# W1's gradient with the layer gradient held and u moved, each tile turned afterwards, in a fused backward kernel on one core

## The chip, the core and the metric

The kernel runs on one core of one Trainium2 chip. The time is the device time of one launch in microseconds (us). The core has five engines with queues of their own: TensorE (PE, matmuls; its weight loads stand as PEld), VectorE (DVE), ScalarE (ACT), GpSimd (POOL) and SyncE (SP). SP and POOL are used here almost only to issue DMAs. TensorE writes to eight banks (PSUM), and ACT or DVE copies results out of them.

## The reference

The program returns the output of a gated mix of two layers and its gradients by 14 inputs. L = 2048 rows, D = 448, N = 256, F = 1792:

```
g = sigmoid((x * gate_w).sum(-1))                 # x = u, 2048 x 448
a = y + u * Dskip                                 # y: u convolved with K by FFT, K from A, B, C, log_dt
h = x @ w1 + b1                                   # 2048 x 1792
b = (relu(h) ** 2) @ w2 + b2
out = g * a + (1 - g) * b
grads = vjp(out, all inputs but B_x)(grad_out)
```

The part that is changed is one gradient of the dense layer, that of W1 (448 x 1792): x^T times dh, where dh = 2 relu(h) (db @ w2^T) is the layer gradient, 2048 x 1792, and the sum runs over the 2048 rows.

## The kernel before

Everything is in bf16 with sums in fp32. The convolution is made by matmuls with Fourier matrices in two stages (fwd1, fwd2, inv1, inv2), with turns through DRAM between them; K's powers are built on DVE by doubling (tables), multiplied out by small matmuls (kprod), turned and stored (turn), and read back for the gradients by A, B and C (gradient, with zunit, zq, l1, zq2, l2; then params). The dense layer is worked in 14 tiles of 128 features: pass1 makes h, its square and W2's gradient (dw2), pass2 makes dh and W1's gradient (dw1), and project makes the two projections (y, and the gradient by x) between and after them.

In pass2, for layer tile j: dh of the tile (features by 2048 rows) comes from `layer` and a product on DVE, is stored to DRAM for the second projection, and is turned by `turn_tile` in 16 pieces into `hn`, 128 rows by 16 by 128 features, of which there is one buffer. dw1 of tile j - 1 uses hn before the next turn fills it. It makes four output tiles of (up to) 128 inputs by 128 features: for each of the four, 16 matmuls with u's 128 x 128 piece held and hn's piece moved, 128 columns. The last of the four has 64 inputs. All four lie in one bank, and two copies bring them to SBUF, from where two DMAs per two tiles store them.

The order of all this isn't the order of the code. The code records the operations; neighbouring matmuls of one bank are grouped into tasks up to about 1.3 us by a table of costs (`cost`, `build`); and `read` and `emit` take the tasks in the order that the string ORDER gives, with HANDS saying which engine makes each free copy (A for ACT, V for DVE) and issues each free DMA (S for SP, G for POOL), and BANKS where each result lies in PSUM. Dependences are kept by semaphores. So every instruction has one line in the profile, that of `emit` (L499 before, L501 after), and instructions are told apart by shapes and tiles. All of SBUF that is shared over time is one tile, `arena`.

Names in the profile: `arena` is any buffer in SBUF, `banks` any result in PSUM, `ident` the identity matrix; a matmul's form reads rows*columns of the held operand, then rows x columns of the moved one. A turn is a matmul with the identity, and shows as `banks<-ident,arena`.

Of the kernel before, what the change touches and what calls it, by code (L numbers as in the profile page):

```python
# [28 lines left out]
ARENA = 100544  # L29
# [9 lines left out]
    "wwvRvFwAwevQv-wx7pw07rvS1f1g7s4I1E4M4J4K4L4N4O4P74vKv_w6w2wfwyw3160A7D7Jw8wB7G7E73vOvZwS7K7Fw7wTwU7HwPwg3F1I0z2aw91KwQwk2P7M7L7t7u7v7y7x7z7A7N26"
    "w1wlwo7Iwp7B7Cwq2b4G24wi4F7SwC8bwR1MwmwW7Y7P8c8d7Z4H72wVae7w8ead7Qwuaf2c28aj7O7_w41WwF801U1O1Q2dwjakwnwv8fal7T7Uws7V8Z7-wr2h2e8Y9mwh9n9o9r9qw59s"  # L40
    "9uwt2f7W2g8X7R2i818g2k2Q852R86w_7XwYxc8288xdwD2jxewX4QwEwLwHxs892S83wMx9x0wIapwJ8WwNwOxtxvxuxw8-2Jxx2L2M848_909192932H2Iah8axaxAxBwZxb2Kaoagw-x1"
    "anx2x39495969798xOxP87x52FxRxQx6aixS999a9b9c9ex79d9gwKxT9f9ham9j9i9k9l9w9xx8xzwGxf9taqar9vx4xgatxyxEasav9zauac9p9C9D9AxhxUxi9y2l9Exk9Baw9L2may2G"
    "xFax9Ma4yrxl9FyuazaAysb6aDaC9GaByv9NaEaaytyw9RaFaHaIa5aJ1S9Ha69OaG9SaMxmaKaOaNb7b8xqxj9Q9IaPaQb99Jxrbby8a79Ubabcxo9V9Ky5y6y99Tab9PaSbiaRxpa8xCxD"
    "aTbh2pxnaLaWaUaZbdaYa-9WxGyaycy7bIxHaXaVbH2nxXa9xIb39-yxxK2qbJ9_xLb0b2b19Xa1xMbfxVxWyNxNyOxZbka_bjybx-ydblbmbnbobpbq2oa2brbsbtbvbuyPyhbwbybxbBbz"
    "bAbCyKbEbDbFbG2r2syea0bMbey1bLbNxJyLxYz4y3bOy22Oyfyg0E9Yx_y4ynz1z5z2yjykyAyMz3zkzlbPbQzJz6ypa33I2t9ZylzPzmzKyoy02uyi4T4UyBznb4bRbSbUbXyyyzyqyGzL"
    "zoyCzQyDbVyIzM221YcpbYym3KbTz7dOc4zpc5b5yEbg5tbW5ub-yHc6bKb_c72vyT2NbZyQza20yJ2wyFdPdQ5pcqcrcs5qcxdVc1yRcyctcXySc2cazTcYc95vyZcZcbcuzUc0yUcd5wzb"
    "dUyVcey-zqc_yWy_dWz02B2z0wc3cccfyXztyYzu2Ac8z8z9zczd2Czezf1-2xzgzhd0zXd1zVcjd32yzYd2cgcmd4cvzZcAczzWzrzszzzNcBcDcCzA2DzRzizDzEz-dZzjckcnzvzwzBzC"
    "zFzxch2EzGzH4R4S4X4YcldT5rcizO4VA0A1d-dSdRzyz_coA4A5dX4WA2cEcFcGcIcHcJcLcRcKcMcOdLcNcPcQcS3JcTcVcUcWA6d_e05se2e4d5dNdY3Ld8e3AaAezSe1eIeH4ZA3d6d9"
    "d7eKda4-e7e8e950e6e5dbecBiAfAbdceeAgedAcA75xeb4_51ea5AAhef5y5Cehddei5B5zde58Ajdfdg54Ad555E5FeJ57ejencwc-A9egeo5253565b59dF5Del5G5cdGdHdIdq5geL5f"
    "dhdtdrdidjeMdudv5h5jdk5iemep5Idldm5aerdndK5HekeSeO5LdJ5k5M5JdMdoeqAuesevdwdCetexewds5PdzeTAydD5d5eAzAvAw5oeNA85QeyezfgeBeAeCeQeVeUeWeXeYeZeue-e_"  # L50
    "f4f0f1f2f3f5f7f6f8fadx5l5K5YdpAAAk6a5m68zIAidydA696bABAo5RADf95S5T5UdB5O5nAxeDAlApAqAm666EASfbfcfdAT5Nfe67An5V6FAOAPAQ5ZAUhlArAR5-AV5WBjfffhdEAt"
    "fiflfkfmfofnfqfwft5_frfpeF5Xfufxfsfv61As63fy60AEAFAG646ceEfFfG6v6g6265eGhn6whohpeRhqfzfHfAhthrAWfBfjhvf-huhsAH6fhAePfIhzfLfM6dfJhBf_g0g1g76xfC6y"
    "6h6jg6gxgwgygAfOfD6i6GAIAJfNAXhmfPgBgCg3hxAKfU6ofE6k6n6rfQACAN6e6HfV6p6sfRgEfX6qALfK6KgD6t6LfYAMgFhCBA6I6J8h6z6B6AB9hk6uBCAYB0B1B2AZfZfW6m6N6Og4"
    "g96Cg2g8gagcgbgdge6D8jfS6MfTB5B3hDhygf6lggghgigjgkglgqgmgnBagogpB6BbA-BcB7A_6RB8grgs6SBlg5Bk6PBdhwgtgugviggG0ChFhEgJgHBmB46QBnBUBggIhIgKihiigL6U"
    "6W6VhJgMBeBogNhHhehGhKhNgVgOhLhOhfhghPhShUgzij6ZBphMhThYBqhhhRBfgPhW6ThQBzhXgQgR6Xhjik6-gWh-hV6YgXhZgYirisgSBr8iilg_imBsi0i2i1gTiRBVi570BWh0iniS"
    "iTBtBxh2BviViWh3iX6_BhiYiZhigUh1gZBBBHByg-i6BwBIBXh4h_i3BEBFCgBDi8i7ibiaBLh8BJh5i4i-hbChiphci9h6BuBM8lBGit8niuivixiwiyiziAiBBNBSBQC0C1h9BZBRBTBY"
    "C4C58m8kBPhdBOh7BKCiiCiDB-CBC6C7C2iEB_CfCDiGiFiIC3iHCdiLiJ8UC9iKiMiNCACCCbC8iOiP8o8p8q8w8x8y8rCc8s8z8Vhaio0yCkCejUicCn8AiQjFieid8t8uCoCl8BCY2Tje"
    "8C8vifiqiUCZjfjgjhi_CmCanSobCXj0j5j2j38Ej68F8Gji8D8MGbof8N8Ojzj1Cpj4j7k38PC-nRDg8HjAjBjCjbjDjJnUj8jkjl8QCIjjj98IjmjajcCFCGCJk8k9jdCHnPCjCrCsCqnT"
    "jECtDh8JDiCK8K8RjIohnXnZCwnYCyCvjtn-jnoECuCzju8SCxjooejpn_o0jqnVCEnWCMCNCOo20Bjro1CLCTogk4jXp1k5jYkajZCPDjCVCQCWo3jwo4oFkbo6CUoojvDDo5omj-onCSo7"
    "o8j_jxnQ8ToaopD0CRokjsjyD3oljGk0jHoDD1D4D2DooiDlojDpDmjKoGo9k6k7D5D6DYp2C_D7D8D9DcorDbocoqDnp0osDqotqgDaodDEjLDdjNDFoujMjPjTjRjOjVpTDeDfovjWowoH"  # L60
    "oIDkjSkdoxDsDLoJjQDtkooKk1DroyDuDZDwkgDvkhD-DGkikkDMkjp3kcDyD_keklozDIDBDzDNkfoADJDCDKHyk2kyE1DxE2E3DAE4E5E6EFkrEGktkvkukDkskxkwkEkJknkpkqkFkmkz"
    "oLkAEEoMkTE7oNoBDHDPDQDRoOoPoCoQkGkOkPkBE_kQk-DOpVGlk_oZDTkCDSkRDUDWDXkWkKpUkYkZoUkXDVqFoVkMkSkUEHpSkLoWoRoSp6oToXE0p7kNkHE8oYkIkVl1p8pap4E9Eap9"
    "EhpbEjp5pcpdqhEcEfEgEJEMEkEKENl0EbEOqfEdo-o_pepfEeELEipQpYphp-piqipZq0pgq1l2Elpjp_l3l4EnpWEvEwppqGpmExl5plpkl7pXq2Eol6q3l8pnpRpoldEplbl9q4lcqjEq"
    "Ezq5ErEyEsqklelJlfq6lhqElaqHEtlgq7q8EmlmlllMliq9lQlRlOlnlNlPlolpECqpF0lqEuljFklur2lrqqqlqmlkltEDqnlvlxlwlyqbF1EAlCF7lsFllSF8qoshlBlAlzlFEBEIqamo"
    "lKlTlGEQr4F4lDlEF5qsF9qcFmlIqrqdqwqOqPqBqxqtquF6qMlHqemxqyERqvqIlVqzEPr1ESmyqAqJEXqCqKqNF2lUlYlLr3EYEUlWqDqLEZlZETEVlXForUm0E-mtmrm1m4mumsFGl-qQ"
    "m5Fpm2EWFrFsq-qRmvm3qVmwr9Fqm9rbqSraFam7qTFtrc8Lr5r6m8mambmcmgr7mdqWF3r8m6l_FbrWrTFcFdFiFeqUmfFgmhqXreFhFHmkFIqZmpmen3mimlFjmjrdmzmnmmrRFfsgFNFK"
    "FLFnFvqYmAFwFxq_FOG6FMFzFBsGFyG7FPrVsjFAmBmDmCFCmErirjmIrkr0FErfrgFDrhrXFFmHmJmqmLmKrYr_mMrmmGmFmNrZs1s0Gcr-rlFJFRJQmQs2n6n8namPFSn7n9mTGdmUmRs3"
    "FTrnroFWs4Genbs5mSmXsisdFYmYFZs6FXFUs8mOsFrSs9sas7FVsbGfn4skmZsHslm-sIm_n0soF-smspscrpFQsqF_mVn1pxmWn2nesnFut3nfsrstG0G1ssuincniG2ngnjseG3sxndsN"
    "nhsfsuG8tVG5nlsOsvsyswn5sLsMnnsPsCnmsJsKGmszsAG4t2tUGonqnrnosQsBsRsSsDnpnvnusTsUnynwt4t5sWGpnzsVG9sEnDnxsXtanCnGGGGasYtbnEt6sZnFnstXt8t7nBnHs_nJ"
    "s-nInAtWt9tctdGhujtetfuhGjGwukt0GnGinttStgthtitjtotkpqtltYtZu0prpspyu1t-pwpvpLpKtmpNrqpMt_u2GkGgGzGyptu3pGpupztrpCpDpFpEtnpAtpnkt1GrGDpHu5GuGxu4"  # L70
    "rrGErxrwtTrvtqpBv8pIGsu9pOrLuruarMGtpJupruusrtv7u6uqubu7rsrNu8ultsv9unrDumueuorzrArOucpPrEudGFuGuuutrGGOrytwGBufrFvbrHvdrCGCGPrIrBrKuytvrPtytzuD"
    "uvuwtxtutMrJnLGqGvuztNGRuAuxtEtFuguCuBvattGSuEtItOtPtQtAuHGKuFuMu_v6uNuOv0v1v2v3vcnKuLtJGHuJuIGQtBtHtGGUtLGItCtKtDJRuKuTuUGLrQuPHxH3uXuQv4GTuVuW"
    "H4GNuYGJtRHzH0uRHAHBuSnMH1HCnOH6H2nNGYHDHFGVHGHHHIHEGWHJHMHTHKHUu-HVGZuZG_H5HWJSGXJTGMHXHLHZHhHeH-HYH_I0I1I4HfIbHiIcIdJUIeIfHaHbI2IgHgHSHRGAv5Ih"
    "IiIjHkH7HcI7I3H8IkIlIoIvIaIwIxH9HNI8ImHdHrI5IyIsHuIzIrItIBHjIAHsHvICHPIDIEHQHlIGI6IuI9IFIIIJIKInINHtHmIMILHoG-HwIHIOHnIpIqHOIRIPHpJJHqJIJKJHIQIS"
    "IWIUIVIXJ1J2J3J4IYJ8J5J6J7JfJ9JgJhJiITJaI_J0JmJkJlJnJvJoJjJeJdI-JpJqIZJtJuJyJwJAJzJxJcJrJBJCJDJsJFJEJGJLJMJNJOJbJP")
HANDS = (
    "AAAVGSAAAASSAAAAGSAAAAGSAVAVAVVVAAVAVAVAVVVVAVVVVAAVAAAVAVVAAAVAAAAAGSAAAASGAAAAGSAAAASSVAAAVASAAAASGSSSAVAAVVAVAAAVAAAAAAVVAVAAAAAVAAAAVAAVAASA"
    "AAAAAAAAASSAASSGSAAAAAAAAAASGAASSGSAAAAAAAAAAGSAASGAAAAAAAAAAGGAAGSVAAVAGAGAGASASVSVGAGASASGGGGSSSAGAGASVSVGVSVGAGAVAVVASAGAGASVGVGVGASVGVGAAAAA"
    "AAAAAAAVAVAAVVAVVVVAAAAAVVVVAAAAVGVAAAASAGVSVSASVSAGAGASASVVVAAGAGVSVGVGVSAGAGASAGAAVVAVAAAAAAVVVAAAAVAVVVAAVAAAAAAAAAAAGVAVAAGAGAGVGAGVSASAGASA"
    "SVAVAVSAGAGVSAGAGVSAGASASAAAAAAAAAAAAAAAAAVAAAVVVAAAVVAAAAAAAAVSAVAAVSASVGVSAGVGVSASVSASSSGGVAVVSAAVVSGGAAAVGVAVASGSAAVAGAAAAGSGAAAVGAVAVSGGSGAA"  # L80
# [184 lines left out]
class Order:  # L265
# [95 lines left out]
    def cost(self, it):  # L361
# [5 lines left out]
        if eng == "PE":  # L367
# [5 lines left out]
            if "tile_position" in k:  # L373
                c = max(1, 128 // max(rows, 32 if rows <= 32 else 64)) * (4 if cols <= 32 else 2 if cols <= 64 else 1)
# [146 lines left out]
def kernel(ctx, tc, A_u, A_A_re, A_A_im, A_B_re, A_B_im, A_C_re, A_C_im, A_log_dt, A_Dskip,  # L521
# [39 lines left out]
    def bank(n=1):  # L561
        return order.banks(n)
# [966 lines left out]
```

## Time and profile before

| | |
|---|---|
| three runs | 714.98, 716.46, 716.55 us; median 716.46 |
| profiled execution | 715.82 us, span from first to last instruction 714.0 |
| granted TensorE clock | 0.978 |
| busy | PE 662.6, PEld 409.0, DVE 544.8, ACT 426.6, POOL 155.7 us |
| DMA | 191.42 MB, 268 GB/s |

A busy share is an average over stages; which engine bounds a stage is read from the busy times of that stretch and from the waits in it. A group's mean length is that of one instruction from start to end; matmuls overlap, so a matmul's price in a row is the group's busy time divided by its count.

### The profile page before, as it was taken

How to read it: one execution, taken by the hardware profiler on the slowest of the kernel's cores; microseconds unless marked ns; L12 is line 12 of the kernel's file. 1: busy time of each engine (PE TensorE's matmuls, PEld its weight loads, DVE VectorE, ACT ScalarE, POOL GpSimd, SP SyncE). 2: the span in 40 equal slices, each digit the busy share in tenths (PEclk: the TensorE clock that was granted, in tenths of full speed). 3: DMA queues.
4: the chain of work that ended last, by engine and by line, in shares of the span. 5: the costliest groups of instructions: out<-in, count | busy, mean ns of one | idle time of the engine just before them, and what ended most of it. 6: DMA issues, size and time to landing. Idle time of an engine off the chain costs nothing.

```text
span 714.0 us, 18735 instructions
## 1 busy us (share of the span) xinstructions
PE 662.6 (93%) x7864; PEld 409.0 (57%) x7864; DVE 544.8 (76%) x918; ACT 426.6 (60%) x638; POOL 155.7 (22%) x262
## 2 busy tenths in 40 slices
PE   2876999999999899888999999999999998899997
PEld 1432564655754545436788866775657675564442
DVE  3589978899798798798983775478877879982652
ACT  4599978989778667656531534436573766651012
POOL 3001222130220122133122212311221031333122
PEclk9989979999999899999999999999999999999998
DMA  8946556568788987899989988997988888999796
GB/s 173 259 148 221 194 192 216 202 242 295 252 259 336 336 281 267 279 329 318 374 270 290 285 273 264 351 298 260 303 273 267 246 234 283 293 280 344 263 294 179
DMA packets 94190, 191.42 MB, mean 268 GB/s; under 512 B 18327, under 2 KB 64793, under 8 KB 91417
## 3 DMA queue, kind: packets, MB, share of 16 engines
q0 software_dynamic: 22320, 93.70, 40.2%
q1 hardware_dynamic: 70488, 89.12, 40.2%
q10 hardware_dynamic: 1296, 7.41, 2.5%
q8 instruction: 61, 1.00, 0.6%
q14 instruction: 25, 0.20, 0.1%
HBM read 104.81 MB, written 85.38 MB: 266 GB/s over the span
## 4 chain that ended last, share of the span: by engine, by line
PE 63%; DMA 14%; DVE 8%; issue 6%; ACT 6%; SPq 1%; POOL 1%; POOLq 0%; DVEq 0%; ACTq 0%
PE banks L499 63%; DVE arena L499 8%; ACT arena L499 6%; DMA arena<-in_A_u_dram 3%; DMA arena<-hd 2%; DMA arena<-c_Ek 2%; DMA arena<-yt_d 1%; DMA hd<-arena 1%; DMA arena<-drT_d 1%; DMA arena<-dk_d 1%; DMA arena<-fb_d 1%; SPq L499 1%; DMA yt_d<-arena 1%; DMA arena<-in_A_C_re_dram 1%; POOL arena L499 0%
## 5 line engine op out<-in xcount | busy, mean ns | idle before, releaser
L499 PEld LDWEIGHTS <-arena 128*128 128x128 bf16 (+4 forms) x6798 | 349.4, 106 | 227.3 <-issue 98.9
L499 PE MATMUL banks<-arena 128*64 128x16 bf16 (+11 forms) x5300 | 433.4, 257 | 18.1 <-ACT arena L499 12.6
L499 DVE TENSOR_TENSOR arena<-arena 128x512 bf16<-128x512 bf16 (+11 forms) x526 | 374.6, 749 | 29.9 <-PE banks L499 11.1
L499 ACT CAST arena<-banks 128x896 bf16<-128x896 f32 (+6 forms) x293 | 213.4, 763 | 201.4 <-PE banks L499 169.4
L499 ACT COPY arena<-banks 128x1024 bf16<-128x1024 bf16 (+3 forms) x129 | 115.1, 917 | 51.6 <-PE banks L499 50.5
L499 PE MATMUL banks<-ident,arena 128*128 128x128 bf16 (+2 forms) x1354 | 115.5, 230 | 19.4 <-DMA arena<-in_A_A_re_dram 7.4
L499 DVE CAST arena<-banks 128x448 bf16<-128x448 f32 (+8 forms) x63 | 48.4, 778 | 39.3 <-PE banks L499 27.5
L499 DVE COPY arena<-banks 128x1024 bf16<-128x1024 bf16 (+4 forms) x58 | 35.2, 616 | 45.0 <-PE banks L499 35.8
L499 DVE SCALAR_TENSOR_TENSOR arena<-banks,arena 128x1024 bf16<-128x1024 f32 (+1 forms) x44 | 44.0, 1003 | 20.7 <-PE banks L499 13.7
L499 PE MATMUL banks<-arena,ident 128*128 128x512 bf16 (+2 forms) x352 | 58.3, 294 | 0.0
L499 POOL DMA_DIRECT2D yt_d<-arena x36 | 19.9, 553 | 135.3 <-ACT arena L499 96.4
L499 PE MATMUL banks<-arena,MI 64*128 64x448 bf16 x384 | 43.0, 360 | 2.9 <-DVE arena L499 1.8
L499 ACT ACTIVATE arena<-arena 128x512 f32<-128x512 f32 (+5 forms) x68 | 42.5, 648 | 3.6 <-DVE arena L499 3.6
L499 POOL DMA_DIRECT2D out_dram<-arena x44 | 25.1, 572 | 61.1 <-ACT arena L499 41.1
L499 PEld LDWEIGHTS <-ident 128*128 128x128 bf16 x352 | 26.2, 98 | 19.1 <-issue 6.4
L499 ACT ACTIVATE arena<-banks,pcol 128x1024 bf16<-128x1024 f32 x27 | 29.7, 1131 | 4.0 <-PE banks L499 2.0
L499 PEld LDWEIGHTS <-MI 64*128 64x128 bf16 x384 | 17.6, 96 | 21.3 <-issue 7.3
L499 ACT CAST arena<-arena 128x512 bf16<-128x512 f32 (+2 forms) x52 | 25.2, 503 | 0.4 <-ACT arena L499 0.4
L499 POOL DMA_DIRECT2D arena<-in_B_w_dram x26 | 16.2, 624 | 32.2 <-PE banks L499 31.9
L499 PE MATMUL banks<-arena,negI 128*128 128x512 bf16 (+2 forms) x100 | 22.1, 308 | 0.2 <-DVE arena L499 0.2
L499 PE MATMUL banks<-arena,F 64*128 64x448 bf16 x64 | 12.7, 418 | 6.1 <-ACT arena L499 3.0
L499 DVE SCALAR_TENSOR_TENSOR arena<-arena 128x256 f32<-128x256 f32 (+1 forms) x44 | 16.9, 385 | 0.9 <-ACT arena L499 0.7
(100 smaller groups left out, 247.9 us busy)
## 6 DMA issues: line engine op xcount, KB each, us to landing
arena<-yt_d POOLq DMA_DIRECT2D x10, 1280.0 KB, 9.3
yt_d<-arena POOLq DMA_DIRECT2D x36, 256.0 KB, 3.1
yt_d<-arena SPq DMA_DIRECT2D x34, 256.0 KB, 4.5
hd<-arena SPq DMA_DIRECT2D x34, 224.0 KB, 5.5
sp<-arena ACTq DMA_DIRECT2D x8, 896.0 KB, 6.3
gd<-arena SPq DMA_DIRECT2D x14, 448.0 KB, 4.7
arena<-gd SPq DMA_DIRECT2D x7, 896.0 KB, 7.0
arena<-hd SPq DMA_DIRECT2D x7, 896.0 KB, 7.8
```

The lines of the kernel that those rows point to most:

```text
L499: getattr(real[t["on"]], op)(*a, **k)
```

## The change

Now hn's piece (128 rows by 128 features) is held and u's whole row block, 448 columns, is moved: 16 matmuls of 448 columns per layer tile, in two halves of eight, give the tile's gradient features by inputs, 128 x 448, in one bank. It is copied to a new SBUF buffer (`dwT`, 448 wide), turned by four matmuls into a second bank, and copied out from there in the two pieces as before. The arena grows by 448 columns, and the row that collects log_dt's gradient sums (`row8`) shares the tile of an early result (`row13`). In `cost`, the packing factor for small matmuls is capped at four, which groups the last inverse stage's matmuls as 5 or 6 into a task as before but costs them more in the planner. The tables ORDER, HANDS and BANKS are new throughout; one line of the first stands for them.

```diff
-ARENA = 100544
+ARENA = 100992
 ORDER = (
-    "0D0g09000e0i0f2U0h0a01022W040c03350F2V36380J2X39373a3b070G0L3c3d0H0d0b0805060k0K1j1t1r0Ivf0M1h3f3e0q0P1v1x1k3g0Q1n1i0m0l0n0j0p2-2Y320s2_2Z1p331u"
+    "090g000f0h0i0e0D0102040305070608350n0j0c0k2U2W0H0L0o0m0l0a0d2X0F2V0b0E36383a37393b0I0Gvg0P1j1v3c3d3e0M0p3f3g3i1w1k3h3j1h0u0J1p1r1i0Kve0Tvf1l1s1q"
...
-                c = max(1, 128 // max(rows, 32 if rows <= 32 else 64)) * (4 if cols <= 32 else 2 if cols <= 64 else 1)
+                c = min(4, max(1, 128 // max(rows, 32 if rows <= 32 else 64)) * (4 if cols <= 32 else 2 if cols <= 64 else 1))
...
-    fix = dict(Wt=1792, ..., dws=2 * D, UT=7168, ...)
+    fix = dict(Wt=1792, ..., dws=2 * D, dwT=D, UT=7168, ...)
...
-    def dw1(j, dt):
-        z = P if dt < 3 else 64
-        if dt == 0:
+    dwTb = put_at("dwT", D)
+
+    def dw1(j, th):
+        if th == 0:
             tmp2["dw"] = bk(bank())
         ps = tmp2["dw"]
-        for t in range(LT):
-            T_.matmul(ps[0:z, P * dt:P * dt + P], lhsT=U2[:, t, P * dt:P * dt + z], rhs=hn[:, t, :], start=(t == 0), stop=(t == LT - 1), skip_group_check=True)
-        if dt == 3:
+        for t in range(8 * th, 8 * th + 8):
+            T_.matmul(ps[:, 0:D], lhsT=hn[:, t, :], rhs=U2[:, t, :], start=(t == 0), stop=(t == LT - 1), skip_group_check=True)
+        if th == 1:
+            w = dwTb
+            E_.evac(w, ps[:, 0:D])
+            ps = bh(bank())
+            for dt in range(4):
+                z = P if dt < 3 else 64
+                T_.transpose(ps[0:z, P * dt:P * dt + P], w[:, P * dt:P * dt + z], ident[:])
             b = tmp2["d1"][:, :, P * (j % 2):P * (j % 2) + P]
             evac(b[:, 0:3], ps[:, 0:384].rearrange("p (a f) -> p a f", a=3))
             evac(b[0:64, 3], ps[0:64, 384:512])
...
                 if j > 0:
                     dw1(j - 1, 0)
-                    yield 0.9
+                    yield 1.5
...
             if j > 0:
-                for dt in range(1 if j < FT else 0, 4):
-                    dw1(j - 1, dt)
-                    yield 0.9
+                for th in range(1 if j < FT else 0, 2):
+                    dw1(j - 1, th)
+                    yield 1.5
...
-    row8 = cst("row8", D, p=1)
+    row8 = row13
```

What the listings of the order show, at three places. On TensorE, at the last layer tile, before: the passage from the third to the fourth output tile of W1's gradient (the shapes are those of the result, inputs by features; the fourth has 64 inputs).

```order
L499 LDWEIGHTS arena
L499 MATMUL banks<-arena 128x128
L499 LDWEIGHTS arena
L499 MATMUL banks<-arena 64x128
L499 LDWEIGHTS arena
```

The same place after: the end of the 448-column matmuls, six matmuls of a gradient step (l1), the four turns, and what comes behind them.

```order
L501 MATMUL banks<-arena 128x448
L501 LDWEIGHTS ident
L501 MATMUL banks<-arena,ident 128x512 [waits Activation_49]
...
L501 LDWEIGHTS negI
L501 MATMUL banks<-arena,negI 128x512 [waits DVE_49]
...
L501 LDWEIGHTS arena [waits Activation_49]
L501 MATMUL banks<-ident,arena 128x128
...
L501 MATMUL banks<-ident,arena 64x128
L501 LDWEIGHTS arena [waits DMASW0_49]
L501 MATMUL banks<-arena 128x128 [waits DVE_49]
```

The turns wait for ACT's copy of the tile, and the next gradient step's matmuls stand behind them.

On ACT, the last two layer tiles before: the pieces 128x3x128 and 64x128 are W1's gradient going out of a bank (the others copy fwd2's and inv1's results, 128x896, and those of the gradient steps).

```order
L499 COPY arena<-banks 128x1024
L499 CAST arena<-banks 128x3x128
L499 CAST arena<-banks 128x512
L499 CAST arena<-banks 128x32x32
L499 CAST arena<-banks 128x896 x2
L499 CAST arena<-banks 128x32x32 x3
L499 CAST arena<-banks 128x3x128
L499 CAST arena<-banks 128x896
L499 CAST arena<-banks 64x128
```

The same after: 128x448 is the last tile's copy before its turns, and the two pieces on either side of it are those of the last tile but one (above) and the last (below).

```order
L501 CAST arena<-banks 128x896
L501 COPY arena<-banks 128x3x128
L501 COPY arena<-banks 64x128
L501 CAST arena<-banks 128x448
L501 CAST arena<-banks 128x896
L501 CAST arena<-banks 128x32x32
L501 COPY arena<-banks 64x128
L501 COPY arena<-banks 128x3x128
L501 CAST arena<-banks 128x32x32 x2
```

The last tile now passes ACT three times where it was two, with two other copies between the first and the second.

On POOL, the end of the program before: in_A_u_dram is the reload of u for the last sum (its other three DMAs are SP's).

```order
L499 DMA arena<-drT_d 128x3584
L499 DMA out_dram<-arena 32x2x896 x7
L499 DMA arena<-hd 128x4x896
L499 DMA out_dram<-arena 32x2x896
L499 DMA arena<-in_A_u_dram 32x7168
L499 DMA out_dram<-arena 32x2x896 x9
```

The same after:

```order
L501 DMA out_dram<-arena 32x2x896 x3
L501 DMA arena<-drT_d 128x3584
L501 DMA out_dram<-arena 32x2x896 x4
L501 DMA arena<-in_A_u_dram 32x7168 x3
L501 DMA out_dram<-arena 32x2x896 x10
```

Three of the reload's four DMAs have moved from SP to POOL.

More of the change, by code (lines that the diff above doesn't have):

```diff
@@ L39 @@
[L39 to L62, printed above, removed]
@@ L1443 @@
     A.put("UT")
-    A.put("DB", "dbuf", "dws", "w1p")
+    A.put("DB", "dbuf", "dws", "dwT", "w1p")
     D_.dma_start(outb.rearrange("p t d -> p (t d)"), bass.AP(tensor=y_d, offset=0, ap=[[LT * D, P], [1, LT * D]]))
```

88 lines of the change are left out of this document (57 added, 31 removed).

## The prediction

> **What bounds the kernel now.** I read the page first, then the busy times by stretch, then TensorE's waits, then the groups by shape, and last the timeline and the chain at the end.
>
> ```profile
> span 714.0 us, 18735 instructions
> PE 662.6 (93%) x7864; PEld 409.0 (57%) x7864; DVE 544.8 (76%) x918; ACT 426.6 (60%) x638; POOL 155.7 (22%) x262
> PE 63%; DMA 14%; DVE 8%; issue 6%; ACT 6%; SPq 1%; POOL 1%; POOLq 0%; DVEq 0%; ACTq 0%
> ```
>
> TensorE (PE) is busy for 93% of the span and makes 63% of the chain that ended last. But the share is a mean over stages, so the stretches matter (busy us and, in brackets, instructions of PE, PEld, DVE, ACT, POOL; then granted clock, DMA share, GB/s):
>
> ```profile
> 20.00:80.00 60.00, 49.83 (x344) 23.91 (x343) 49.74 (x101) 50.89 (x74) 5.08 (x9) 0.94 0.70 212
> 80.00:340.00 260.00, 246.01 (x3212) 144.71 (x3210) 224.25 (x383) 200.02 (x309) 55.77 (x97) 0.97 0.78 268
> 340.00:580.00 240.00, 239.18 (x3269) 173.55 (x3268) 174.18 (x254) 117.42 (x169) 50.84 (x78) 0.99 0.88 286
> 580.00:640.00 60.00, 54.65 (x585) 35.79 (x583) 54.79 (x81) 34.85 (x50) 17.80 (x28) 1.00 0.99 279
> 640.00:714.00 74.00, 67.65 (x437) 28.45 (x435) 35.30 (x94) 13.51 (x28) 19.27 (x34) 0.97 0.85 273
> 38.00:80.00 42.00, 31.85 (x238) 14.54 (x238) 38.15 (x78) 41.97 (x60) 5.08 (x9) 0.92 0.59 186
> ```
>
> From 38 to 80 us ScalarE (ACT) is full: 41.97 of 42. From 80 to 340 us three engines share the bound. From 340 to 580 us TensorE is idle for 0.8 us of 240, at the full clock, while ACT has 122.6 us free and DVE 65.8. In 580 to 640 us DVE and TensorE are both at 91%. TensorE's waits, in total, times, longest, first over the whole span and then, in the last two rows, of 340 to 580 us alone:
>
> ```profile
> PE banks L499 <- ACT arena L499: 17.4, 23, 1.9
> PE banks L499 <- DVE arena L499: 4.4, 6, 1.2
> ...
> PE banks L499 <- DMA arena<-c_Ek: 0.4, 1, 0.4
> PE banks L499 <- DMA arena<-hd: 0.3, 1, 0.3
> ```
>
> In that long stretch TensorE waits for no other engine at all. W1's gradient is made there: its 64 matmuls of a layer tile are the runs of 128 columns such as 343.02 and 567.63 in the timeline below. The first layer tile's begin near 343 us and the last one's end near 581 us, so what TensorE saves on them shortens the stretch one for one.
>
> **The change part by part.** Removed are 14 x 48 matmuls of form 128*128 with 128 moving columns and 14 x 16 of form 128*64. Added are 14 x 16 of 128*128 with 448 columns, and 14 x 4 turns (matmuls with the identity moving, 42 of them 128*128 and 14 of 128*64). The groups of these forms:
>
> ```profile
> L499 PE MATMUL banks<-arena 128*128 128x128 bf16 x1232 | 76.9, 219 | 0.7 <-ACT arena L499 0.5
> L499 PE MATMUL banks<-arena 128*64 128x128 bf16 x224 | 15.1, 220 | 0.0
> L499 PE MATMUL banks<-arena 128*128 128x448 bf16 x676 | 141.2, 355 | 5.4 <-ACT arena L499 3.5 <-DMA arena<-drT_d 1.6 <-DMA arena<-hd 0.3
> L499 PE MATMUL banks<-ident,arena 128*128 128x128 bf16 x1254 | 103.6, 229 | 19.4 <-DMA arena<-in_A_A_re_dram 7.4 <-DMA arena<-in_A_C_re_dram 4.2 <-issue 2.5
> L499 PE MATMUL banks<-ident,arena 128*64 128x128 bf16 x70 | 13.7, 257 | 0.0
> ```
>
> The mean of one (219 ns) is its length through the pipeline; the price in a row of many is busy time over count. The first group holds 672 of ours: 76.9/1232 = 62.4 ns, so 41.9 us. The second is ours alone: 15.1 us. Removed: 57.0 us. The third group is W2's gradient and the projections, the same shape as the new matmuls: 141.2/676 = 209 ns, and 224 of them are 46.8 us. Turns: 103.6/1254 = 83 ns, 56 of them 4.6 us. Sum on TensorE: 46.8 + 4.6 - 57.0 = **-5.6 us**. The saving is plain: 512 output columns per position step become 448, as the last, half-filled tile of 64 features no longer costs a full pass.
>
> The ends of these prices, from the timeline (start, us, form, count):
>
> ```profile
> 343.02 1.96 PE L499 MATMUL banks<-arena 128*128 128x128 bf16 x32
> 567.63 1.08 PE L499 MATMUL banks<-arena 128*64 128x128 bf16 x16
> 640.91 1.49 PE L499 MATMUL banks<-arena 128*128 128x448 bf16 x7
> 642.65 2.82 PE L499 MATMUL banks<-arena 128*128 128x448 bf16 x14
> 300.39 1.07 PE L499 MATMUL banks<-ident,arena 128*128 128x128 bf16 x16
> ```
>
> Seven more matmuls of 448 columns take 1.33 us, 190 ns each: 42.6 us. Sixteen turns in 1.07 us are 67 ns each: 3.7 us. With 61 ns (1.96/32) and 67.5 ns (1.08/16) for the removed ones, 41.2 + 15.1 = 56.3: best case -10.0 us. Worst: 14 of the turns at the 196 ns of the 128*64 group (13.7/70) and 42 at 83, together 6.2, and 448 columns at 213 ns (1.49/7), 47.7: with 56.3 removed, -2.4 us. I take -5.6, from the groups, which stand nearest to a mean over all places.
>
> Added copies. Each turned tile must leave its bank twice: 14 copies of 128x448, of which the tables put 10 on ACT and 4 on DVE, and of the 28 pieces copied out in both programs 18 are on ACT now and 10 on DVE, where it was 21 and 7.
>
> ```profile
> L499 ACT CAST arena<-banks 128x448 bf16<-128x448 f32 x57 | 30.6, 537 | 67.4 <-PE banks L499 56.4 <-DVE arena L499 10.2 <-ACT arena L499 0.8
> L499 DVE CAST arena<-banks 128x448 bf16<-128x448 f32 x21 | 12.8, 618 | 4.3 <-PE banks L499 2.7 <-ACT arena L499 1.4
> ```
>
> That is 10 x 0.537 = 5.4 us on ACT and 4 x 0.618 = 2.5 us on DVE, in a stretch where they have 122.6 and 65.8 us free: nothing on the path. If that cover were gone it would be 7.9 us.
>
> The new wait. The four turns wait on TensorE for the copy of the tile; behind them everything on TensorE is queued, and the banks it would fill. In the order the shortest distances are at the last layer tile (six matmuls of 512 columns between the last 448-column matmul and the turns), the second (four matmuls and eight turns) and the eighth (six matmuls, sixteen turns); elsewhere more stands between. Six matmuls at 0.2 us cover 1.2 us; a copy is 0.54 us, and one other copy (a piece of the tile before) is queued ahead of it on ACT. Both fit, so I count 0; if the longest wait of the table above (1.9 us) came at all three places, it would be 5.7 us.
>
> A half of the turned layer gradient is free after 8 of 16 matmuls now, where each of the four column passes used to read all of it. TensorE does not wait there, so this is worth 0, at best the 0.7 us of the two waits left.
>
> The row that the tail shares with an early result is written only after the early store has been issued; between them TensorE has over 30 us of work: 0. No DMA is added or removed.
>
> The end of the span. The reload of u is released by the last projection, and the last 16 matmuls need it:
>
> ```profile
> 691.98 0.33 SPq L499
> 692.31 0.05 issue
> 692.36 0.41 SPq L499
> 692.78 0.05 issue
> 692.83 13.04 DMA arena<-in_A_u_dram
> 705.87 0.14 issue
> 706.00 4.88 PE banks L499 x16
> ```
>
> Before, three of its four DMAs are issued by SP and one by POOL; now three by POOL. One such issue on POOL is
>
> ```profile
> L499 POOL DMA_DIRECT2D arena<-in_A_u_dram x4 | 2.1, 516 | 2.8 <-PE banks L499 2.8
> ```
>
> so the last starts about 3 x 0.52 = 1.5 us after the first instead of 0.85 + 0.4: I add 0.5 us (from 0 to 1.5).
>
> All else in the tables, hands and banks moves too. The TensorE work ahead of the last matmul for the convolution's powers, and of the first gradient step, differs from before by under 5 us by the listings. I take 0 for it, with the PE waits of the first 340 us as the size of what can go wrong (below).
>
> **Sum.** -5.6 + 0.5 = -5.1 us. The profiled execution took 715.82 us with a span of 714.0; so 710.7. The median of the runs, 716.46, is 0.64 above it: 711.3.
>
> **Against the change: turns.** Sixteen turns in 1.07 us at a granted clock of 0.99 to 1.00 say 67 ns each. [...]
>
> **The rivals.**
> A, my forecast: TensorE's saving goes through. 711.3; with its prices at their ends -10.0 - 0.7 and -2.4 + 1.5, so 705.8 to 715.6.
> B, the freed time turns into waiting. The later gradient steps on DVE and the reads of the stored powers set the pace from 574 to 640 us anyway; TensorE arrives early and waits there. For: DVE and TensorE are both at 91% in 580:640. Against: between 340 and 580 us DVE has 65.8 us free and follows TensorE. Price: the saving is lost, 716.5 to 717.0 (with the 0.5).
> C, slower: the new order of the first 340 us lays the copies out of the banks less well. Place: 20 to 340 us, where ACT is full at first and PE's waits for ACT are 15.5 of the 17.4 us. A wait there is 15.5/19 = 0.82 us.
>
> ```profile
> PE banks L499 <- ACT arena L499: 15.5, 19, 1.9
> ```
>
> Seven more such waits eat the 5.6 us; nine more make it slower by 0.3%; if they double to 38, +15.5 - 5.1 gives 726.9. Its centre is 14 more, 11.5 - 5.1 = +6.4: 722.9. For: all tables are new. Against: the same work stands ahead of the same points in both.
> [...]
>
> **How the numbers follow.** A 0.58, B 0.15, C 0.22, D 0.05. A measurement of this kernel can tell about 0.3%, 2.1 us, from no change. So faster 0.58, same 0.15, slower 0.27. The range begins at 704.5, which is A's best, 705.8, less the some 0.2% by which runs of one kernel differ (714.98 to 716.55 before), and reaches to 721.0, over B, D and the nearer part of C; what is left out is the farther part of C and a little below A.
>
> **What would show it.** Right: in the profile after, a group 128*128 128x448 of 900 at about 0.2 us of busy time each, PE's sum 5 to 6 us lower, again no wait for ACT or DVE in the long full stretch, the last projection 5 to 6 us earlier. Wrong: the turns as the instruction before which TensorE idles; PE's waits for ACT above 23 us; a first projection of the second pass, or the last matmul of the powers (383 us before), later than before; a row of 56 more turns that raises the group's mean busy time above 150 ns.

## The result, and the profile after

The changed kernel took 705.56 us (median of four runs, 704.99 to 707.15), the kernel before beside it 715.72 (714.93 to 716.55): a ratio of 0.986, 95% interval 0.984 to 0.988, or 10.2 us. The prediction had the sign and the range, but half the size. Ratios, means and distances in this document leave out the runs that took over 1.5% longer than the fastest of their kernel on the same chip, 33 of the 124 of the kernel before that stand beside the experiments and none of the changed kernel's 22, while medians hold all runs.

The first lines of the page of the changed kernel (span; busy time of each engine; shares of the chain that ended last):

```profile
span 703.9 us, 17514 instructions
PE 659.3 (94%) x7248; PEld 382.5 (54%) x7248; DVE 544.8 (77%) x916; ACT 435.4 (62%) x654; POOL 156.8 (22%) x265
PE 72%; DVE 10%; ACT 7%; DMA 6%; issue 3%; POOL 0%; SPq 0%; ACTq 0%; DVEq 0%; POOLq 0%
```

The span is 10.1 us shorter, but TensorE is busy for only 3.3 us less (662.6 before). The rest, 6.8 us, is idle time: span less busy time was 51.4 us and is 44.6. The busy times by stretch, with the columns as before the change:

```profile
20.00:80.00 60.00, 49.56 (x335) 23.05 (x334) 50.32 (x100) 54.20 (x80) 10.20 (x19) 0.89 0.52 162
80.00:340.00 260.00, 248.22 (x3212) 145.42 (x3210) 221.65 (x384) 198.46 (x302) 54.45 (x91) 0.96 0.85 282
340.00:580.00 240.00, 239.44 (x2720) 150.85 (x2720) 182.27 (x258) 126.48 (x188) 52.01 (x79) 1.00 0.91 295
580.00:640.00 60.00, 55.64 (x572) 35.66 (x571) 51.76 (x86) 33.91 (x51) 19.11 (x33) 1.00 0.97 285
640.00:703.90 63.90, 57.57 (x368) 23.23 (x366) 29.59 (x77) 12.80 (x26) 16.06 (x29) 1.00 0.82 258
```

The long stretch is as full as it was (0.6 us idle of 240), with 8 to 9 us more of copies and other work on each of DVE and ACT. TensorE's only waits in it:

```profile
PE banks L501 <- ACT arena L501: 0.3, 1, 0.3
PE banks L501 <- DVE arena L501: 0.2, 1, 0.2
```

The first of them is one tile's turns waiting for ACT's copy (timeline, with the wait ahead of the row in brackets):

```profile
355.57 0.50 PE L501 MATMUL banks<-ident,arena 128*128 128x128 bf16 x4 [0.33 <-ACT arena L501]
```

The turns of the other 13 tiles wait for nothing. The groups by shape that the sum was made of:

```profile
L501 PE MATMUL banks<-arena 128*128 128x448 bf16 x900 | 189.8, 354 | 0.7 <-DMA arena<-drT_d 0.7
L501 PE MATMUL banks<-ident,arena 128*128 128x128 bf16 x1296 | 107.9, 227 | 12.0 <-DMA arena<-in_A_A_re_dram 4.3 <-DVE arena L501 3.4 <-ACT arena L501 1.5
L501 PE MATMUL banks<-arena 128*128 128x128 bf16 x560 | 37.3, 219 | 0.0
L501 PE MATMUL banks<-ident,arena 128*64 128x128 bf16 x84 | 17.2, 257 | 0.0
```

By these groups the change removed 54.7 us (76.9 + 15.1 - 37.3) and added 56.4 (48.6 + 4.3 + 3.5), which would be a loss. A group's busy time counts the tail of the last matmul in every run of its kind (0.17 us in the row at 538.20 below: 3.20 us long, 3.03 to the next start), and the new form breaks such runs up differently, so groups can't price the change. From start to next start no tail is counted. One tile before (its 64 matmuls; next row: what follows), in the timeline:

```profile
536.77 3.85 PE L499 MATMUL banks<-arena 128*128 128x128 bf16 x64
540.56 1.12 PE L499 MATMUL banks<-ident,arena 128*128 128x128 bf16 x17
```

and in the changed kernel the four turns of one tile, the 16 matmuls of the next, and what follows:

```profile
537.76 0.50 PE L501 MATMUL banks<-ident,arena 128*128 128x128 bf16 x4
538.20 3.20 PE L501 MATMUL banks<-arena 128*128 128x448 bf16 x16
541.23 0.61 PE L501 MATMUL banks<-ident,arena 128*128 128x128 bf16 x8
```

540.56 - 536.77 = 3.79 us before; 541.23 - 538.20 = 3.03 and 538.20 - 537.76 = 0.44 after, 3.47 together. Summed from start to next start over the records of all 14 tiles it is 52.8 us before and 49.4 after (matmuls 43.2, turns 6.2): **the form is worth 3.4 us**, not 5.6.

The stretch up to 345 us, ahead of nearly all of W1's gradient (before, then after), and TensorE's waits for ACT's copies in it after (15.5 us in 19 waits before, the prediction's row):

```profile
0.00:345.00 345.00, 306.12 (x3633) 174.29 (x3634) 285.38 (x499) 263.53 (x398) 68.54 (x124) 0.97 0.78 254
0.00:345.00 345.00, 311.61 (x3621) 175.08 (x3621) 286.07 (x503) 264.42 (x395) 72.55 (x128) 0.95 0.80 257
...
PE banks L501 <- ACT arena L501: 12.8, 15, 3.1
```

38.9 us are idle before and 33.4 after: 5.5 us less at a place where little but the tables differs, 2.7 of them in waits for ACT's copies. But the granted clock was 0.97 there before and 0.95 after, and at the halved clock TensorE is busy longer with the same work (a turn took 106 ns, against 56 at full clock: last section), so not all of the 5.5 us need be time gained (experiment 4). And at the end the last 16 matmuls, which need u again, wait for nothing:

```profile
696.48 3.19 PE L501 MATMUL banks<-arena,ds_b 128*1 128x448 bf16 x16
```

Before, they took 4.88 us (the prediction's row at 706.00) after a wait of 1.62, and for most of them the granted clock was 0.50 (last section). The three pieces, 3.4 + 5.5 + 3.3, make 12.2 against 10.1 of span, so some of it was lost again, or is chance. The experiments had to tell which.

### The profile page after: what moved, and what is told of

Its sections match the earlier page's. It is cut to its first block, busy times and chain, and to the rows that moved or that the text cites. A ratio compares the mean times of both kernels' runs of the same rounds, so it can differ in the third digit from the quotient of the medians.

```text
span 703.9 us, 17514 instructions
## 1 busy us (share of the span) xinstructions
PE 659.3 (94%) x7248; PEld 382.5 (54%) x7248; DVE 544.8 (77%) x916; ACT 435.4 (62%) x654; POOL 156.8 (22%) x265
## 4 chain that ended last, share of the span: by engine, by line
PE 72%; DVE 10%; ACT 7%; DMA 6%; issue 3%; POOL 0%; SPq 0%; ACTq 0%; DVEq 0%; POOLq 0%
PE banks L501 72%; DVE arena L501 10%; ACT arena L501 7%; DMA arena<-sp 1%; DMA arena<-y_d 1%; DMA arena<-in_A_u_dram 1%; DMA arena<-drT_d 1%; DMA hd<-arena 1%; DMA arena<-in_A_A_im_dram 1%; POOL out_dram L501 0%; SPq L501 0%; ACT L501 0%; ACT rows L501 0%; ACTq L501 0%; ACT g_b L501 0%
## 5 line engine op out<-in xcount | busy, mean ns | idle before, releaser
L501 PEld LDWEIGHTS <-arena 128*128 128x128 bf16 (+4 forms) x6182 | 322.3, 106 | 232.3 <-issue 94.3
L501 PE MATMUL banks<-arena 128*64 128x16 bf16 (+10 forms) x4628 | 431.0, 270 | 8.5 <-ACT arena L501 3.9
L501 DVE TENSOR_TENSOR arena<-arena 128x1024 bf16<-128x1024 bf16 (+14 forms) x525 | 373.8, 750 | 25.8 <-ACT arena L501 13.0
L501 ACT CAST arena<-banks 128x896 bf16<-128x896 f32 (+4 forms) x289 | 213.8, 770 | 152.0 <-PE banks L501 131.1
L501 ACT COPY arena<-banks 128x1024 bf16<-128x1024 bf16 (+5 forms) x155 | 126.3, 838 | 77.0 <-PE banks L501 62.0
L501 PE MATMUL banks<-ident,arena 128*128 128x128 bf16 (+1 forms) x1410 | 122.1, 228 | 12.0 <-DMA arena<-in_A_A_re_dram 4.3
L501 DVE COPY arena<-banks 128x1024 bf16<-128x1024 bf16 (+5 forms) x60 | 34.5, 582 | 45.0 <-PE banks L501 29.9
L501 DVE CAST arena<-banks 128x448 bf16<-128x448 f32 (+4 forms) x53 | 46.1, 878 | 24.2 <-PE banks L501 17.0
L501 ACT ACTIVATE arena<-arena 128x256 bf16<-128x256 f32 (+5 forms) x69 | 43.8, 655 | 1.7 <-PE banks L501 1.3
L501 PE MATMUL banks<-arena,F 64*128 64x448 bf16 x64 | 13.2, 418 | 14.1 <-ACT arena L501 7.7
L501 POOL DMA_DIRECT2D hd<-arena x20 | 12.9, 646 | 54.7 <-ACT arena L501 51.2
```

What stands on the lines that cost most here:

```text
L501: getattr(real[t["on"]], op)(*a, **k)
```

## The experiments

**How runs are compared.** The kernel before was run beside every experiment: 91 runs on five chips, from 705.6 to 717.4 us, mean 712.5. Its first four runs (714.9 to 716.6), which are not among the 91, lie in the upper part of that spread. The time goes with the mean granted TensorE clock that each run lists:

| granted clock | runs of before | mean us |
|---|---|---|
| 0.985 and over | 23 | 709.6 |
| 0.980 to 0.985 | 35 | 712.5 |
| 0.977 to 0.980 | 12 | 713.7 |
| under 0.977 | 21 | 714.8 |

A line through the 91 falls by 4.1 us for 0.01 of clock, with 2.1 us of scatter about it. In the tables below, "at equal clock" is a kernel's mean distance from that line, with its standard error; the ratio is of plain times. Comparing at equal clock takes it that the line of the kernel before holds for the other kernels too, which was not shown.

**1. The changed kernel again**, unaltered, on two chips.

> The changed kernel unaltered, as the measure for the runs beside it: 0.986 of before, as in its first measurement, with TensorE idle for about 45 us and busy for 659.

> The changed kernel unaltered, beside the next one on the same chip: 705 to 707 us.

| | median us | ratio to before | at equal clock |
|---|---|---|---|
| first measurement | 705.56 | 0.986 (0.984 to 0.988) | -8.0 +- 0.5 |
| again | 706.84 | 0.991 (0.987 to 0.994) | -8.0 +- 0.2 |
| again, beside the wide turns | 707.08 | 0.993 (0.990 to 0.997) | -8.0 +- 0.5 |

The changed kernel is the steadier one: 22 runs, mean 706.5. Plainly it gains 6.0 us on the mean of the 91 runs of before, at equal clock 8.0. Over all 124 runs of before but one of 774.1 us, the mean is 714.2, the plain gain 7.7, and 9.4 at equal clock by a line through these; so 8.0 is known to about 2 us. The first 10.2 held some 2 to 4 us of before's spread.

**2. TensorE's time passes through.** More turns, with nothing moved:

```diff
-            for dt in range(4):
+            for dt in (0, 1, 2, 0, 1, 2, 0, 1, 2, 3):
```

> The changed kernel with ten turns for each tile in place of four (the first three are made three times over), nothing moved. Six more turns at 56 ns on 14 tiles are 4.7 us of TensorE. Theory one, TensorE sets the pace there and the time passes through: 4.7 us more than the changed kernel, 0.994 of before. Rival, the freed or spent time is taken from waits at 560 to 660 us: 2 us more or less. Rival, every shift against the tables brings new waits and half-clock windows: 7 us or more.

710.98 us, 0.9945 (0.991 to 0.998), at equal clock -3.1 +- 0.6: 4.9 us above the changed kernel for 4.7 us of turns. That is theory one: TensorE's time passes through. The page's busy times:

```profile
PE 664.9 (93%) x7332; PEld 387.6 (54%) x7332; DVE 545.1 (77%) x916; ACT 435.6 (61%) x654; POOL 156.3 (22%) x265
```

The other side, 4 of the 64 matmuls of a tile left out of the kernel before, which leaves its sum incomplete:

```diff
-        for t in range(LT):
-            T_.matmul(..., stop=(t == LT - 1), skip_group_check=True)
+        lt = LT - 4 if dt == 1 else LT
+        for t in range(lt):
+            T_.matmul(..., stop=(t == lt - 1), skip_group_check=True)
```

> The kernel before, with 4 of the 64 matmuls of each tile of W1's gradient left out (the second column tile sums 12 of 16 position tiles): TensorE has 14 x 4 x 59 ns = 3.3 us less to do, which is what the trace gives for the whole change of form, and not one instruction is moved. Theory one (the form's saving goes through one for one): 3.3 us less than before. Rival, the saving turns into waiting between 574 and 640 us: 0 to 0.5 us less. Rival, a saving of TensorE's time there is worth more than itself because what follows meets fewer waits: 8 to 10 us less.

713.67 us, 0.997 (0.993 to 1.001), at equal clock -1.5 +- 0.5. Of 3.3 us 1.5 came through; where the rest went was not settled.

**3. The narrow turn.** First with the fourth turn shifted, and its rows copied from partitions 64 to 127; the second kernel differs only in where three unread loads stand.

```diff
-                z = P if dt < 3 else 64
-                T_.transpose(ps[0:z, P * dt:P * dt + P], w[:, P * dt:P * dt + z], ident[:])
+                c0 = min(P * dt, D - P)
+                T_.transpose(ps[0:P, P * dt:P * dt + P], w[:, c0:c0 + P], ident[:])
...
-            evac(b[0:64, 3], ps[0:64, 384:512])
+            evac(b[64:128, 3], ps[64:128, 384:512])
...
```

> The changed kernel with the fourth turn of each tile as wide as the others: it holds columns 320 to 447 and not 384 to 447, and its lower 64 rows are copied from partitions 64 to 127 (three loads that nothing reads move behind the last tile). Theory: the step from a held operand of 128 columns to one of 64 is what makes the four turns 0.44 us in place of 0.22; each tile saves 0.21 us, 14 of them 3.0 us, 702.6 us. Rival: the time hangs on the copy or on the bank behind the fourth turn, or on the step back: no more than 0.5 us, 705.0 to 705.6.

714.72 us, 1.004 (1.000 to 1.008). The turns did fall to 0.22 us a tile, but the three loads stood in GpSimd's queue ahead of one that TensorE needed (its waits from 580 to 640 us):

```profile
PE banks L501 <- DMA arena<-in_B_w_dram: 7.6, 1, 7.6
```

> The changed kernel with the fourth turn as wide as the others, as in the run of wide turns, but with the three loads that nothing reads put where GpSimd's queue has nothing urgent behind them. In that run the four turns of a tile took 0.22 us in place of 0.44, but a load of W1 came 7.6 us late. Theory: with the load in time again the saving of 2.9 us shows, 0.982 of before and 2.9 us below the changed kernel beside it. Rival: it turns into waiting at 580 to 640 us, no more than 0.5 us below the changed kernel.

708.91 us, 0.993 (0.989 to 0.996), at equal clock -6.6 +- 0.6: 1.4 us worse than the changed kernel. The load was in time (TensorE waits 0.7 us for it); TensorE now waited elsewhere:

```profile
623.01 0.38 PE L501 MATMUL banks<-arena,ident 128*128 128x128 bf16 x4 [2.19 <-ACT arena L501]
647.17 0.36 PE L501 MATMUL banks<-arena,negI 128*128 128x448 bf16 x1 [1.82 <-DMA arena<-y_d]
```

The first of these waits the changed kernel doesn't have; at the second it waits 1.4 us too. That is how the prediction's rival B would look, in the one profile of this variant; that these waits took the whole saving is not shown. Then the same turn with nothing moved at all: it reads 64 columns on, into the next buffer, and the extra rows are not copied out.

```diff
-                z = P if dt < 3 else 64
-                T_.transpose(ps[0:z, P * dt:P * dt + P], w[:, P * dt:P * dt + z], ident[:])
+                T_.transpose(ps[0:P, P * dt:P * dt + P], view(w, P * dt, [[1, P]]), ident[:])
```

> The changed kernel with the fourth turn as wide as the others by reading on past its tile: it holds columns 384 to 511, of which the last 64 belong to the next buffer, and only the 64 rows that are wanted are copied out. Nothing else is changed or moved. Theory: 0.22 us a tile, 2.9 us in all, and with TensorE setting the pace 2.9 us less than the changed kernel, at the same granted clock 12.5 us less than before. Rival (a little less work meets waits for copies and loads at 600 to 660 us that it had just covered, as in the other run with wide turns): 0 to 1 us less than the changed kernel.

> The changed kernel with the fourth turn as wide as the others by reading on past its tile, once more, now beside the changed kernel. Theory: 2.9 us less than it, 702.5 to 704. Rival: the saving is lost in waits at 600 to 660 us in most executions, no more than 1 us less.

704.16 us, 0.990 (0.986 to 0.994), and on the other chip 703.39, 0.989 (0.983 to 0.995), against 707.08 for the changed kernel beside it. The means there differ by 3.6 +- 1.0 us (standard error); at equal clock it is -10.4 and -11.1, short of the 12.5 expected. This version beats both kernels. Its rows of the same tiles:

```profile
534.17 0.39 PE L501 MATMUL banks<-ident,arena 128*128 128x128 bf16 x4
534.39 3.19 PE L501 MATMUL banks<-arena 128*128 128x448 bf16 x16
```

0.22 us for four turns, 55 ns each, in place of 0.44.

**4. The tables ahead of W1's gradient.** The order, engines and banks of one kernel up to the first of its matmuls, of the other from there on, both ways; and the same with a seam at 88 us.

```
before_new_until_dw1: program of before; tables of after to 342 us, of before from there on
after_old_until_dw1:  program of after; tables of before to 342 us, of after from there on
old_front, before_new_front: the same, with the seam at 88 us
```

> The kernel before with the changed kernel's order, engines and banks up to the first matmul of W1's gradient (about 342 us, the first 1543 tasks; ten or so small tasks lie on the other side of the seam), and its own from there on. No work is changed, and none of W1's gradient lies ahead of the seam. Theory one (half of the gain is idle time that the new tables take out of the first 345 us): TensorE's idle time up to 345 us falls from 39 to 33 or 34 us, and the end comes 5 us earlier than before, 0.993. Rival (the gain is the form's, the early idle time is made up later): within 1 us of before.

> The exchange the other way: the changed kernel with the order, engines and banks of before up to the first matmul of W1's gradient, its own from there on. Theory one: idle time up to 345 us near 39 us in place of 33, and the end 5 us later than the changed kernel, 0.993 of before. Rival: within 1 us of the changed kernel, 0.988.

> The changed kernel with the order, engines and banks of before up to W2's third gradient tile (about 88 us, the first 365 tasks of before), and its own from there on. TensorE idled 24.9 us up to that point before and 21.6 after. Theory one: the 3.3 us come back as they are, 708.9 us. Rival: the front's idle time is made up later, since the three engines share the bound from 80 to 340 us: 705.6 to 706.5.

> The kernel before with the changed kernel's order, engines and banks up to W2's third gradient tile (about 88 us), and its own from there on; no work is changed. Theory one: TensorE idles 3.3 us less up to there, and the end comes 3 to 5 us earlier (the exchange the other way, measured beside before, gave back 4.2 us of idle time and 2.7 us of busy time in its trace). Rival, the idle time is made up later: 0 to 1 us.

| | median us | ratio to before | at equal clock |
|---|---|---|---|
| before, new tables to 342 us | 713.18 | 0.999 (0.996 to 1.002) | -1.4 +- 0.7 |
| after, old tables to 342 us | 715.27 | 0.999 (0.995 to 1.002) | +1.5 +- 0.8 |
| after, old tables to 88 us | 713.12 | 0.999 (0.996 to 1.002) | -1.4 +- 0.4 |
| before, new tables to 88 us | 724.49 | 1.016 (1.012 to 1.021) | +6.3 +- 0.9 |

The stretch up to 345 us in the first two:

```profile
0.00:345.00 345.00, 309.06 (x3656) 175.65 (x3657) 286.57 (x502) 265.13 (x398) 71.25 (x127) 0.96 0.79 257
0.00:345.00 345.00, 304.13 (x3617) 172.79 (x3618) 286.65 (x504) 262.93 (x397) 70.96 (x128) 0.98 0.79 256
```

35.9 and 40.9 us idle. Over the profiles of all kernels here that keep one order up to there, the idle time up to 345 us is 38.0 us on average with the order of before (7 profiles, 35.3 to 40.9) and 35.0 with the new one (11, 33.4 to 36.2): 3.0 us less, whichever form follows. Part of that is the clock. Half of the time that TensorE was busy at the halved clock is counted as lost to it, after the prices of a turn at the two clocks, 106 and 56 ns (last section): in the traces 10.7 us up to 345 us on average with the order of before and 13.2 with the new one. Over the 18 profiles idle time falls by 0.32 +- 0.08 us for each us lost so, and at equal loss **the early tables take out 2.2 +- 0.5 us of idle time**. In time the first exchange shows less of it and the second far more (9.5 us worse than the changed kernel). Some of both is the seam: in the second, TensorE waits just behind it (345 to 580 us),

```profile
PE banks L501 <- ACT arena L501: 3.2, 2, 2.0
PE banks L501 <- DVE arena L501: 2.6, 1, 2.6
```

where neither whole kernel has such a wait; and the new front in the old kernel waits 6.2 us once, at 103 us in its profile, some 15 us behind its seam:

```profile
PE banks L499 <- issue: 6.7, 2, 6.2
```

So the runs show that the early tables matter, and not to the microsecond how much.

**5. Form and tables apart.** Each form in the other's tables, all through.

```
form_old_tables:     program of after; tables of before for all common work
old_form_new_tables: program of before; tables of after for all common work
```

> The changed program (gradient held, u moved, four turns) with the order, engines and banks of before for all work that both programs have; the new matmuls stand where the first two column passes stood, the turns at the fourth pass or, where that is nearer, at least 2 us of TensorE work behind the last matmul of their tile. The trace says that the new form takes 49.4 us of TensorE (224 matmuls at 193 ns, 56 turns at 110 ns) where the old took 52.8. Theory one, the gain has two sources: the form is worth 3.4 us, 712.3 us, and TensorE's idle time in the first 350 us stays near 39 us. Theory two, the form brings the whole gain whatever the tables: 705.6. Theory three, the tables alone bring it: 715.7. Forecast on record, the form is worth 5.6: 710.

> The program of before (u held, four column passes) in the changed kernel's order, engines and banks for all work that both have; the four column passes stand at the places of the four matmul tasks of the new form. Theory one: 6.7 of the 10.2 us come from the tables, 709.0 us, with TensorE's idle time in the first 350 us near 33 us. Theory two (all from the form): 715.7. Theory three (all from the tables): 705.6. Forecast on record (tables worth nothing): 716.

740.75 us, 1.034 (1.028 to 1.041), and 737.48, 1.035 (1.029 to 1.041): 25 us slower than before, both. All three theories fell. TensorE's long stretch, first the new form in the old tables, then the reverse:

```profile
345.00:580.00 235.00, 221.72 (x2479) 141.02 (x2478) 158.44 (x236) 103.71 (x154) 45.18 (x71) 0.96 0.82 269
345.00:580.00 235.00, 217.97 (x2949) 155.52 (x2947) 152.65 (x218) 103.91 (x155) 43.63 (x66) 0.98 0.82 265
```

13.3 and 17.0 us idle, where each form in its own tables has under 1; and the waits are for copies:

```profile
PE banks L501 <- ACT arena L501: 6.0, 8, 1.5
PE banks L501 <- DVE arena L501: 4.9, 5, 1.9
...
PE banks L499 <- ACT arena L499: 12.8, 9, 8.2
PE banks L499 <- DVE arena L499: 4.2, 3, 2.2
```

A tile of the new form uses a second bank and one more copy, and in tables made for the other form 5 and 22 of the 603 results that both programs have lie in another bank than in those tables. Whether the banks, the copies or the order do the damage was not told apart. Idle time isn't all of it either: over the whole span the first idles 65.1 us and loses 29.7 to the halved clock, the second 68.1 and 18.9, the kernel before 51.4 and 14.8.

The form's own price shows in all tables, though. TensorE's busy time less what the halved clock cost is 648.8 us on average over seven profiles with the old form (the whole of its matmuls), 645.0 over seven with the new one and its four turns, and 642.2 over the two that read on past the tile. The form is worth 3.8 +- 0.6 us of TensorE's work by this count, 3.4 by the rows; it shortens the program only with tables in which TensorE doesn't wait more for it.

**6. The tail.** The queues that bring u back; u brought back into free memory, so that it needn't wait for the last projection; and the tables from the end of W1's gradient on, exchanged both ways. Between the two kernels two of the four loads of u have changed queues, not three: one of four was GpSimd's, and three are now. With u early, its four loads also stand earlier in the order.

```diff
-HANDS, loads of u in order: S S G S
+HANDS, loads of u in order: G G G S
```

```diff
-    Ut = A.get("Ut", 7168).rearrange(...)
+    Ut = A.get("Ut", 7168, at=90304).rearrange(...)
```

```
before_new_tail: program of before; its tables to the end of W1's gradient, those of after from there on
after_old_tail:  program of after; its tables to there, those of before from there on
```

> The kernel before with one thing changed: of the four loads that bring u back at the end, the first three in order are issued by GpSimd and one by SyncE, as the changed kernel has it (three by SyncE and one by GpSimd before). In the trace of before u landed 13.9 us after its release and the last 16 matmuls waited 1.6 us for it and then ran at half clock (4.9 us in place of 3.2); in the changed kernel it took 12.3 us and nothing waited. Theory (the queues make the difference): no wait there, the last stretch 3 us shorter, 0.996. Rival (the DMA's time hangs on the other traffic at that moment): the wait stays, within 0.5 us of before. My forecast on record, 0.5 us slower.

> The kernel before with u brought back into memory that the gradient steps left free, so that its four loads need not wait for the last projection; they are issued behind the last load of stored states, some 2 us earlier. In the trace of before the last 16 matmuls waited 1.6 us for u and ran at half clock, 4.9 us in place of 3.2. Theory (that wait is the tail's part of the gain): no wait, 1.6 us less than before at the same granted clock, and up to 3.3 with the clock. Rival (the loads then take the DMA from the stores and loads around them): no gain.

> The kernel before with its own order, engines and banks up to the end of W1's gradient (about 580 us; six small tasks lie on the other side of the seam) and the changed kernel's from there on; no work is changed. In the traces TensorE's idle time from 645 us on is 3.2 us before and 0.7 after. Theory: the new tables of the tail are worth 2.5 to 3 us, at the same granted clock 2.5 to 3 us less than before. Rival (the waits of the tail hang on when work arrives there, not on its order): within 0.7 us of before.

> The exchange the other way: the changed kernel with the order, engines and banks of before from the end of W1's gradient on. Theory: 2.5 to 3 us more than the changed kernel, at the same granted clock 7 us less than before. Rival: within 0.7 us of the changed kernel, 9 to 10 us less than before.

| | median us | ratio to before | at equal clock |
|---|---|---|---|
| before, other queues for u | 715.15 | 0.996 (0.990 to 1.001) | -1.0 +- 1.0 |
| before, u early | 715.20 | 1.005 (1.001 to 1.009) | +0.9 +- 0.8 |
| before, new tail | 716.49 | 1.007 (1.003 to 1.010) | +3.2 +- 0.5 |
| after, old tail | 707.03 | 0.996 (0.992 to 0.999) | -7.1 +- 0.5 |

Nothing at the tail gains an amount that can be told from none: the new tail makes before slower, and the old one costs the changed kernel 0.9 us at equal clock, with standard errors of some 0.5 us on either side. With u early the wait for u went, and another came in its place, 2.2 us for a load of stored states at 696 us. Of the 3.3 us that the first pair of traces shows at the tail, 1.7 are those of the halved clock, and they belong to that execution: in the profile of before_less, which has the same tail, the last 16 matmuls took 3.20 us, from 707.97 on.

## Why the prediction was right or wrong, step by step

- **The bound** held. TensorE is idle for 0.6 us in the long stretch, and turns added there cost their own time (experiment 2). Time taken out of the changed kernel's turns came through too (2.9 us by the rows, 3.6 +- 1.0 measured, experiment 3), but matmuls taken out of the kernel before gave back only 1.5 of 3.3 us. One for one holds in the changed kernel's tables, then, and not in every case.
- **The form, -5.6 us:** the first step that failed, by size. Removed were 52.8 us and not 57.0; added were 43.2 and not 46.8, and 6.2 of turns and not 4.6; together -3.4. The group prices held tails (0.17 us in the row at 538.20) that vanish or appear with the neighbours. The best-case price of the new matmuls (190 ns each, from the rows of seven and fourteen) was near the true one (43.2/224 = 193 ns; 3.03/16 = 189 in the row at 538.20, where each has a weight load of its own), and the worst case of the turns, 6.2 us, was theirs, for a reason that the prediction didn't have: the step to a piece of 64 columns and back costs a tile 0.22 us, half of its turns' time (experiment 3).
- **The copies and the turns' wait, 0:** right within 0.3 us. One tile's turns wait 0.33 us for ACT's copy.
- **The early half of hn, 0:** nothing in the trace speaks against it.
- **The reload of u, +0.5:** not there. Its queues make no difference that the runs can tell (experiment 6).
- **All else in the tables, 0:** the second step that failed, and the one that cost the forecast most. Up to 345 us the new tables hold 3.0 us less idle time over 18 profiles, 2.2 at equal loss to the halved clock, and 5.5 in the first pair. The prediction looked there for a loss (rival C) and named the right place and, for 2.7 of the 5.5 us, the right wait, but it compared two points of the order and took an equal amount of work ahead of them for equal waiting.
- **The comparison itself:** the forecast stood on a median of three runs of before, 716.46. Over 91 runs, from 705.6 to 717.4, its mean is 712.5: single runs differ by far more than the 0.2% that the prediction took. Against that mean the changed kernel's gain is 6.0 us; that this lies near the 5.1 forecast is luck, as the sum is another: at equal clock 8.0 = 3.4 for the form + 2.2 for the early tables + 2.4 that no run here assigns. Of the forecast's 5.1, the form gave 2.2 less, the reload took 0.5 less, and the early tables with the unassigned rest gave 4.6 more. The 10.2 us first measured hold 2.2 on top of the 8.0, which are chance in the four runs of before.
- **Rival B** didn't happen in the changed kernel. In two variants (before_less, wide_turn_late) half of a saving and all of one didn't come through, which fits B; only the second's profile has a wait of the kind. **Chance D**, 0.05 for turns that don't overlap, which the range of the forecast takes in, stands on no run: the four turns of experiment 3 take 55 ns each from start to start, 0.22 us together, although a turn lasts 227 ns on average in its group above.

## What to carry to other kernels

Price a change on a full TensorE from start to next start in the timeline, not from busy time over count: a group's busy time holds the tail of every run of its kind, and the change alters the runs. Here the groups gave a loss of 1.7 us (56.4 against 54.7), and the starts a gain of 3.4. A form and the tables of order and banks that were made for it belong together: exchanged, both were 25 us slower than the kernel before. And before a forecast of half a per cent, look how far the runs of the kernel before lie apart, and at which granted clock the profiled one ran.

## What the hardware showed that was not expected

In the profiled runs of before and of the changed kernel the granted clock is halved in stretches of 3.4, 6.8 and 10.2 us (of 6.8 from 245.4 us before and from 329.3 after, at 0.50 both). Three of them in the run of before (the columns are those of the stretches above; the granted clock is the third figure from the end):

```profile
95.20:105.40 10.20, 10.20 (x148) 6.55 (x145) 6.75 (x16) 6.20 (x11) 1.60 (x3) 0.50 0.44 159
371.60:375.00 3.40, 3.40 (x36) 3.24 (x34) 2.10 (x3) 0.56 (x1) 1.15 (x2) 0.51 0.63 203
706.20:709.60 3.40, 3.40 (x11) 1.17 (x10) 0.00 (x0) 0.00 (x0) 1.81 (x4) 0.50 0.76 219
```

TensorE was busy all through them. In the second, 24 turns took 2.54 us from their first start at 371.66 to the next matmul's at 374.20, 106 ns each; at full clock the eight of the changed kernel at 541.23 took 0.45 us, 56 ns each. The last 16 matmuls took 4.88 us, most of them in the third, and 3.19 in the changed kernel, where the clock was 1.00. So each 3.4 us cost an estimated 1.6 (from the turns) to 1.7 (4.88 - 3.19). The stretches fall differently in executions of one program: the mean clock up to 345 us was 0.95 in the changed kernel's first profile, 0.96 in that of after_again and 0.97 in that of after_beside. A mean clock lower by 0.01 is an estimated 7.1 us (0.01 x 714) of TensorE's time; the line through the runs has 4.1, which fits that part of the loss falls on time that would have been idle (0.32 of each us up to 345 us, experiment 4). The stretch at 706.2 follows the wait for u, but ahead of the one at 371.6 TensorE had had no gap for over 11 us:

```profile
360.00:371.60 11.60, 11.60 (x278) 9.15 (x274) 10.23 (x15) 4.90 (x8) 3.05 (x6) 1.00 0.96 287
```

What sets each stretch off, no run here shows.

And a held operand of another width cost time here at the change: 128 to 64 columns and back, 0.22 us in four turns (0.44 against 0.22, experiment 3), while sixteen pieces of 64 in a row (the prediction's row at 567.63, 1.08 us with its tail) cost about what pieces of 128 do (half of the row at 343.02, 0.98).
